# Eight small SBUF regions placed ahead of the load ring in a decode kernel of gated attention and MLP

## The chip, the cores and the metric

The kernel runs on one core of one Trainium2 chip. The metric is the device time of one execution in microseconds (us); the time before is the median of three runs. A profile of one further execution gives the span, from the first to the last instruction, and what each engine and each DMA queue did in it.

## What is computed

One token of 1024 values goes through two branches, and a gate mixes them. Branch A is attention over a cache: 32 query heads in 4 groups share 4 key and value heads, and each of these has 65,536 cached positions of 128 values. Branch B is a small gated MLP. All inputs are bf16. With its shapes filled in, and helper names shortened, the reference is:

```python
x = A_x                                            # [1, 1, 1024]
g = sigmoid((x * gate_w).sum(-1, keepdims=True))

q = (x @ wq).reshape(1, 1, 32, 128).transpose(0, 2, 1, 3)
k = repeat(k_cache, 8, axis=1)                     # k_cache, v_cache: [1, 4, 65536, 128]
v = repeat(v_cache, 8, axis=1)
p = softmax(einsum('bhqd,bhkd->bhqk', q, k) * 128 ** -0.5)
o = einsum('bhqk,bhkd->bhqd', p, v)
a = o.transpose(0, 2, 1, 3).reshape(1, 1, 4096) @ wo

z = gelu(einsum('bsd,df->bsf', x, w_in))           # w_in: [1024, 3584]
z1, z2 = z[..., :1792], layernorm(z[..., 1792:])
h = einsum('ts,bsf->btf', w_sp, z2) + b_sp
b = einsum('bsf,fd->bsd', z1 * h, w_out)           # w_out: [1792, 1024]

out = g * a + (1 - g) * b
```

The keys and the values are 67 MB each, and with the weights 162 MB are read once. Nothing of it is used twice, so the kernel is a stream of loads with work on the engines beside it.

## The kernel before

**SBUF.** All SBUF data lie in one tensor, `arena` (L202), of 128 partitions. `region` (L188) hands out its space by name, in the order of the list at L193, each region rounded up to 16 bf16 elements (32 bytes). `ab` (L204) and `af` (L207) make bf16 and f32 views from a region's offset, so an edit of the list moves the regions and touches nothing else. The program that is built from it puts `arena` at byte 16,512 of every partition, behind 16,384 reserved bytes and four constants of 32 bytes each.

The first region is `RING`, five slots of 16,384 elements (32 KiB per partition each). All large loads land there. `KT` holds two transposed key pieces, `SC` two buffers of scores, `PSB` and `PTSB` the probabilities and their transposes. The rest is small: `QPAD` holds the queries in the form that TensorE takes as weights for the scores, `SEL` and `BM` are selection matrices for the outputs and the maxima, `ONES` and `ONEB` ones in f32 and bf16, `IDB` an identity, `DM` and `M16` belong to the maximum over the heads' rows.

**Loads.** `stream` (L302) is a list of 29 transfers, written out by hand from L339 to L361: wq, K, w_in, K, K, w_out, then K and V by turns, and the output weights wo in six pieces, the last one of them cut in three by `WO_CUT` (L357). Each transfer is 128 rows, one for each partition, of 2,048 to 65,536 contiguous bytes. `issue` (L376) puts a transfer on SP's queue as soon as what lay in its slots has been used; the DMA is at L389. SP issues in the order of the list, and the first two transfers are moved ahead of the program's start barrier (`R.ahead`). Four small loads (x, the gate's weights and two single values, by `small` at L285) go out on ACT's queue in the same way; those of x and of the gate land in `SC`, eight rows of 256 bytes each. The result goes out from `OROW` in eight rows of 256 bytes (L366); a store of the same bytes is issued earlier, before the last load.

**Keys.** For each K transfer `k_piece` (L496) runs four times per 16,384 positions: DVE transposes a quarter of a slot into `KT` (L502), and PE multiplies it with `QPAD`, eight matmuls of 512 columns into `scp` (through `mm`, whose calls have the lines L260 and L262). When the four are through, the slot is free for the next transfer in it. Two such steps fill `scp`, and `score_pair` (L518) copies it to `SC` and takes its maximum.

**Values.** ACT takes the exponentials (L534), DVE transposes them (L539, L542), and `pv_piece` (L544) multiplies them with a V transfer as it lies in the ring, 32 matmuls into `obt`. The `out_` functions scale and sort the result of a group into `OVZ`, where it is ready as weights for wo.

**End.** The last transfers are wo's. `wo_rows` (L689) and `wo_piece` (L705) multiply them piece by piece as they land (L712 for the last four pieces), with a few idle matmuls between (`spin`), DVE casts the sum (L775), and SP stores it.

The order of the instructions on each engine is that of the calls from L733 to L776. `Recorder` finds the waits between them from the names that each operation reads and writes; addresses play no part in it.

Of the kernel before, what the change touches and what calls it, by code (L numbers as in the profile page):

```python
# [138 lines left out]
def bass_gated_mix__gqa_block_cached__mixer_gmlp__decode_kernel(  # L139
# [22 lines left out]
    KC = D // 128  # L162
    FC = FH // 128
    OC = HQ * Dh // 128
# [3 lines left out]
    total = G * NP  # L168
# [3 lines left out]
    QP = 152  # L172
# [15 lines left out]
    def region(name, nbf):  # L188
        nonlocal cur
        OFF[name] = cur  # L190
        cur += (nbf + 15) // 16 * 16

    for name, n in [  # L193
        ("RING", NSUB * SUB), ("KT", NKT * 4096), ("SC", NSC * 2048), ("PSB", 2 * 1024), ("PTSB", 2 * 1024),
        ("QPAD", 4 * QP), ("IDB", 128), ("BM", 256), ("SEL", 16 * 32),
        ("M16", 32), ("MQ", 32), ("XT", KC), ("WB", 2), ("WBB", 4), ("ONEB", 128),
        ("MAXC", 2 * total), ("LP", 2 * total), ("COLS", 2 * 64), ("DM", 64), ("ONES", 256), ("QALL", 128), ("OVZ", 32 * OC + 31), ("E4Z", 128), ("MHALF", 4),
        ("YB", FC), ("OROW", QW),
    ]:
        region(name, n)  # L200
# [608 lines left out]
```

## Time and profile before

| what | value |
|---|---|
| median of three runs | 381.85 us (381.73 to 382.11) |
| span of the profiled execution | 380.3 us |
| time of the median run beyond that span | 1.55 us |
| PE busy | 235.1 us, 62% |
| DVE busy | 204.6 us, 54% |
| ACT busy, POOL busy | 23.3 us and 8.4 us |
| HBM read | 162.01 MB, 426 GB/s over the span |

The profile has one line for a group of instructions: the line of the code, the engine, the operation, what it writes and reads, how many there are, busy time, mean time of one, and the idle time of its engine just before them with what ended it. A "DMA share" is the mean busy share of the 16 DMA engines in a stretch; it can read a little over 1. Beside these views the trace keeps each single DMA packet with its queue, start, length in bytes and duration in whole ns. A row of a load is one packet.

### The profile page before, as it was taken

To read this page: it belongs to the slowest core of one execution; us is meant where nothing else is said; L and a number is where in the kernel's file an instruction comes from. 1 tells how busy PE (TensorE), PEld (TensorE's weight loads), DVE (VectorE), ACT (ScalarE), POOL (GpSimd) and SP (SyncE) were. 2 spreads that over 40 slices of the span, in tenths; PEclk is the share of its full clock that TensorE was granted. 3 is DMA by queue.
4 is the path that set the end of the run, shared out by engine and by line. 5 is a ranking of instruction groups with operands and counts; after the bars stand their busy time and mean duration, and the time that the engine had idled before them with its cause. 6 is when DMAs were issued, how large, how long until landed. Compare 5 with 4: busy or idle time off the path is not lost.

```text
span 380.3 us, 2581 instructions
## 1 busy us (share of the span) xinstructions
PE 235.1 (62%) x1449; PEld 58.1 (15%) x836; DVE 204.6 (54%) x162; ACT 23.3 (6%) x24; POOL 8.4 (2%) x37
## 2 busy tenths in 40 slices
PE   0061388458558924895788138952895884739378
PEld 0010011011111200122112001220121110212015
DVE  4011496778389525965892249745774882312020
ACT  1000000010420000002200000022000000220000
POOL 5000000000000000000000000000000000000000
PEclk9998599696859985998699859995899697958689
DMA  9999999999999999999999999999999999999996
GB/s 435 427 420 400 469 388 438 441 469 431 401 414 441 441 443 427 434 410 424 477 441 434 434 434 414 415 441 441 434 407 433 445 441 441 436 403 424 419 426 262
DMA packets 4254, 162.17 MB, mean 426 GB/s; under 512 B 532, under 2 KB 532, under 8 KB 788
## 3 DMA queue, kind: packets, MB, share of 16 engines
q1 hardware_dynamic: 4208, 162.01, 98.9%
q8 instruction: 9, 0.15, 0.2%
q10 hardware_dynamic: 36, 0.00, 0.0%
q14 instruction: 1, 0.01, 0.0%
HBM read 162.01 MB, written 0.00 MB: 426 GB/s over the span
## 4 chain that ended last, share of the span: by engine, by line
DMA 56%; PE 23%; DVE 18%; ACT 1%; issue 1%; SPq 0%; ACTq 0%; DVEq 0%
DMA arena<-in_A_k_cache_dram 34%; DVE arena L502 15%; DMA arena<-in_A_wo_dram 10%; DMA arena<-in_A_v_cache_dram 8%; PE scp L260 7%; PE scp L262 6%; DMA arena<-in_B_b_sp_dram 5%; PE obt L260 4%; PE obt L262 4%; DVE arena L539 1%; PE fbt L712 1%; PE fbt L660 1%; ACT arena L534 1%; SPq L389 0%; ACTq L288 0%
## 5 line engine op out<-in xcount | busy, mean ns | idle before, releaser
L502 DVE STREAM_TRANSPOSE arena<-arena 128x2048 f32<-128x2048 f32 x64 | 143.0, 2284 | 48.2 <-DMA arena<-in_A_k_cache_dram 32.7
L260 PE MATMUL scp<-arena 128*128 128x512 bf16 (+1 forms) x275 | 112.8, 429 | 87.7 <-DVE arena L502 86.3
L262 PE MATMUL scp<-arena 128*128 128x512 bf16 (+1 forms) x279 | 113.1, 427 | 0.0
L260 PE MATMUL obt<-arena 128*64 128x512 bf16 (+2 forms) x334 | 62.9, 419 | 17.5 <-DMA arena<-in_A_v_cache_dram 17.5
L262 PE MATMUL obt<-arena 128*64 128x512 bf16 (+2 forms) x334 | 62.2, 414 | 0.0
L260 PEld LDWEIGHTS scp<-arena 128*128 128x128 bf16 (+1 forms) x275 | 27.7, 104 | 200.1 <-issue 101.3
L539 DVE STREAM_TRANSPOSE arena<-arena 128x2048 bf16<-128x2048 bf16 x7 | 16.2, 2311 | 28.5 <-PE obt L262 26.4
L534 ACT ACTIVATE arena<-arena 128x2048 bf16<-128x2048 f32 x8 | 16.0, 2002 | 218.6 <-DVE arena L531 195.6
L260 PEld LDWEIGHTS obt<-arena 128*64 128x64 bf16 (+1 forms) x334 | 18.3, 113 | 70.7 <-issue 56.1
L519 DVE TENSOR_SCALAR_CACHE_REDUCE arena<-scp 128x2048 f32<-128x2048 f32 x8 | 18.3, 2292 | 16.0 <-PE scp L262 16.0
L580 PE MATMUL mbt<-arena 128*128 128x128 bf16 x16 | 1.9, 258 | 12.6 <-DVE arena L575 12.6
L542 DVE STREAM_TRANSPOSE arena<-arena 128x1024 bf16<-128x1024 bf16 x2 | 2.5, 1246 | 12.7 <-PE obt L262 12.7
L490 POOL COPY arena<-arena 32x32 bf16<-32x32 bf16 x16 | 3.2, 203 | 234.5 <-PE scp L262 209.7
L568 DVE RECIPROCAL arena<-mbt 128x1 f32<-128x1 f32 x4 | 0.6, 139 | 14.1 <-PE mbt L563 14.1
L531 DVE TENSOR_REDUCE arena<-mbt 128x1 f32<-128x32 f32 x4 | 0.8, 192 | 13.5 <-PE mbt L528 13.5
L437 PE MATMUL mbt<-arena 1*128 1x2 bf16 x1 | 0.2, 158 | 12.3 <-DMA arena<-in_B_b_sp_dram 12.3
L439 DVE COPY arena<-mbt 128x2 f32<-128x2 f32 x1 | 0.2, 160 | 12.3 <-PE mbt L437 12.3
L775 DVE CAST arena<-fbt 36x128 bf16<-36x128 f32 x1 | 0.3, 283 | 11.0 <-PE fbt L712 11.0
L432 PE MATMUL scp<-arena 8*128 8x1 bf16 x8 | 0.7, 199 | 8.7 <-DVE arena L427 8.7
L712 PE MATMUL fbt<-arena 128*32 128x128 bf16 x128 | 4.1, 220 | 0.1
L712 PEld LDWEIGHTS fbt<-arena 128*32 128x32 bf16 x128 | 3.6, 97 | 1.6 <-DMA arena<-in_A_wo_dram 0.8
L467 DVE CAST arena<-obt 97x1024 bf16<-97x1024 f32 x1 | 1.2, 1225 | 4.9 <-PE obt L262 4.9
(91 smaller groups left out, 54.2 us busy)
## 6 DMA issues: line engine op xcount, KB each, us to landing
arena<-in_A_k_cache_dram SPq DMA_DIRECT2D x6, 4096.0 KB, 33.1
arena<-in_A_v_cache_dram SPq DMA_DIRECT2D x2, 4096.0 KB, 26.0
arena<-in_B_w_in_dram SPq DMA_DIRECT2D x1, 7168.0 KB, 30.4
arena<-in_A_wo_dram SPq DMA_DIRECT2D x3, 2048.0 KB, 33.4
arena<-in_B_w_out_dram SPq DMA_DIRECT2D x1, 3584.0 KB, 21.5
arena<-in_A_wo_dram SPq DMA_DIRECT2D x1, 1280.0 KB, 30.3
arena<-in_A_wo_dram SPq DMA_DIRECT2D x1, 512.0 KB, 31.0
arena<-in_A_wo_dram SPq DMA_DIRECT2D x1, 256.0 KB, 30.8
```

The lines of the kernel that those rows point to most:

```text
L260: return e.matmul(*a, **kw)
L262: one = e.matmul(*a, **kw).ins
L467: P("DVE", lambda e: e.tensor_copy(psb[0:97, :], ob[0:97, :]), w=["psb", "ob"])
L490: P("POOL", lambda e, pb=pb: e.tensor_copy(vw(qpad, 24 + 32 * pb, [[QP, 4], [1, 8]], 32 * pb, 32), vw(qall, 8 * g, [[32, 4], [1, 8]], 32 * ...
L502: P("DVE", lambda e: e.transpose(ktb(i).bitcast(F32), sl[:, 4096 * p:4096 * (p + 1)].bitcast(F32)), r=keys[4 * p:4 * p + 4], w=[("kt", i % ...
L519: P("DVE", lambda e: e.tensor_scalar(scs(j), scp[:, :], 0.0, None, op0=ALU.add, op1=ALU.max, accum_out=maxc[:, j:j + 1]), w=[("sc", j % 2) ...
L534: P("ACT", lambda e: e.activation(psb2, scs(j), ACTF.Exp, bias=gcol(j // 2, K_NB), scale=SCALE, accum_out=lp[:, j:j + 1]), r=[("sc", j % 2 ...
L539: P("DVE", lambda e: e.transpose(ptsb2, psb2), r=["psb"], w=[("ptsb", 0), ("ptsb", 1)])
L542: P("DVE", lambda e: e.transpose(ptsb(n), ab("PSB", 1024, 1024 * (n % 2))), r=["psb"], w=[("ptsb", n % 2)])
L580: ins = e.matmul(mb[:, 0:128], sel[:, 128 * c:128 * (c + 1)], osc[:, 128 * c:128 * (c + 1)], start=(c == 0), stop=(c == 3))
L660: ins = e.matmul(fb[32 * b:32 * (b + 1), 0:QW], e4z[0:97, 31 - j:63 - j], part[0:97, QW * s:QW * (s + 1)], start=(first and s % (NW // 2) ...
L712: ins = e.matmul(fb[32 * b:32 * (b + 1), 0:QW], ovz[:, z:z + 32], sl[:, o:o + QW], start=False, stop=(i == 3 and c == 7), tile_position=(0 ...
```

## The change

Only the list of regions changes. Eight regions that stood behind the large ones now stand ahead of `RING`; the others keep their order.

```diff
     for name, n in [
+        ("QPAD", 4 * QP), ("SEL", 16 * 32), ("BM", 256), ("ONES", 256), ("IDB", 128), ("ONEB", 128), ("DM", 64), ("M16", 32),
         ("RING", NSUB * SUB), ("KT", NKT * 4096), ("SC", NSC * 2048), ("PSB", 2 * 1024), ("PTSB", 2 * 1024),
-        ("QPAD", 4 * QP), ("IDB", 128), ("BM", 256), ("SEL", 16 * 32),
-        ("M16", 32), ("MQ", 32), ("XT", KC), ("WB", 2), ("WBB", 4), ("ONEB", 128),
-        ("MAXC", 2 * total), ("LP", 2 * total), ("COLS", 2 * 64), ("DM", 64), ("ONES", 256), ("QALL", 128), ("OVZ", 32 * OC + 31), ("E4Z", 128), ("MHALF", 4),
+        ("MQ", 32), ("XT", KC), ("WB", 2), ("WBB", 4),
+        ("MAXC", 2 * total), ("LP", 2 * total), ("COLS", 2 * 64), ("QALL", 128), ("OVZ", 32 * OC + 31), ("E4Z", 128), ("MHALF", 4),
         ("YB", FC), ("OROW", QW),
     ]:
         region(name, n)
```

In bytes from the start of a partition (16,512 is the start of `arena`):

| region | before | after |
|---|---|---|
| QPAD | 221,312 | 16,512 |
| SEL, BM, ONES | 223,296; 222,784; 225,312 | 17,728; 18,752; 19,264 |
| IDB, ONEB, DM, M16 | 222,528; 224,544; 225,184; 224,320 | 19,776; 20,032; 20,288; 20,416 |
| RING | 16,512 | 20,480 |
| KT, SC, PSB, PTSB | 180,352; 196,736; 213,120; 217,216 | each 3,968 more |
| MQ to COLS | 224,384 to 224,928 | 640 to 896 more |
| QALL to OROW | 225,824 to 228,512 | as before |

The arena's size stays 212,352 bytes.

## The prediction

> **What bounds the kernel now.** I read the page's slices, its DMA queues and its chain first, then a table by stage, then the end of the timeline, and last the single DMA packets of the trace.
>
> ```profile
> span 380.3 us, 2581 instructions
> ...
> DMA  9999999999999999999999999999999999999996
> ...
> q1 hardware_dynamic: 4208, 162.01, 98.9%
> ...
> DMA 56%; PE 23%; DVE 18%; ACT 1%; issue 1%; SPq 0%; ACTq 0%; DVEq 0%
> ...
> L502 DVE STREAM_TRANSPOSE arena<-arena 128x2048 f32<-128x2048 f32 x64 | 143.0, 2284 | 48.2 <-DMA arena<-in_A_k_cache_dram 32.7
> ...
> arena<-in_A_k_cache_dram SPq DMA_DIRECT2D x6, 4096.0 KB, 33.1
> ```
>
> The DMA engines are busy in every slice but the last. SP's queue q1 alone takes 98.9% of 380.3 us, 376.1 us on each of 16 engines, for 162.01 MB. The chain of waits names PE and DVE for 41%, but the first line of it is still DMA, and L502, DVE's largest group, stands idle 32.7 us for K loads. K transfers of 4096 KB need 33.1 us from issue to landing where their bytes need 9.7 (4,194,304 bytes at 16 times the 27.1 bytes per ns of one engine, below): 23 us of that is queueing, so the next transfer is there before the last one is through.
>
> ```profile
> core 0: us, PE busy (x) PEld busy (x) DVE busy (x) ACT busy (x) POOL busy (x), PEclk, DMA share, GB/s
> 0.00:1.00 1.00, 0.00 (x0) 0.00 (x0) 0.00 (x0) 0.00 (x0) 0.18 (x4) 1.00 0.20 66
> 1.00:96.00 95.00, 46.24 (x276) 10.71 (x152) 51.11 (x58) 3.17 (x5) 5.75 (x21) 0.86 1.01 434
> 96.00:368.00 272.00, 178.74 (x1004) 42.32 (x529) 153.20 (x103) 19.06 (x18) 2.43 (x12) 0.83 1.00 431
> 368.00:378.00 10.00, 9.50 (x160) 4.77 (x147) 0.00 (x0) 1.02 (x1) 0.00 (x0) 0.83 0.88 366
> 378.00:380.30 2.30, 0.67 (x18) 0.32 (x12) 0.28 (x1) 0.00 (x0) 0.00 (x0) 1.00 0.01 1
> ```
>
> By stage the DMA share is 1.00 or 1.01 from 1 to 368 us while no engine passes 66%. So the kernel is one unbroken stream of 376 to 377 us, with 1.0 us ahead of it and some 2.4 behind it. The end hangs on it too:
>
> ```profile
> 373.69 1.79 PEld L712 LDWEIGHTS fbt<-arena 128*32 128x32 bf16 x64 [0.66 <-DMA arena<-in_A_wo_dram]
> ...
> 378.27 0.23 PEld L712 LDWEIGHTS fbt<-arena 128*32 128x32 bf16 x8 [0.18 <-DMA arena<-in_A_wo_dram]
> 378.79 0.28 DVE L775 CAST arena<-fbt 36x128 bf16<-36x128 f32 x1 [11.04 <-PE fbt L712]
> 379.10 0.31 SPq L366 DMA_DIRECT2D out_dram<-arena  x1
> ```
>
> PE's weight loads wait for the last pieces of wo (0.66 and 0.18 us), and what follows the last one is fixed. What the stream gains or loses, the end gains or loses nearly whole.
>
> **The packets.** Every row of a load is one packet: 29 transfers of 128 rows over 16 engines are 232 rows per engine. The shortest packets last 2418 ns for 65,536 bytes, 1213 for 32,768, 159 for 4,096, 84 for 2,048. The first two give 1205 ns for 32 KiB, 37.66 ns per KiB (27.2 bytes per ns). That leaves, beyond the bytes, 8.0, 7.9, 8.4 and 8.7 ns: a row costs its bytes plus some 8.5 ns, whatever its length. This bounds the whole case. A cost at each 4096-byte border inside a row would show in the slope or grow from 2 KiB to 64 KiB; it doesn't. Only a cost per row is left to be saved.
>
> **The change, part by part.**
> (1) No instruction, wait, byte or transfer is added or removed: 0.
> (2) The rows' start. The program puts the arena at byte 16,512 of each partition, which is 4 x 4096 + 128, and RING is its first region. The eight regions hold 608 + 512 + 256 + 256 + 128 + 128 + 64 + 32 = 1984 elements, 3968 bytes; RING goes to byte 20,480 = 5 x 4096. Slots are multiples of 4096 bytes, but for the last two pieces of wo (10,240 and 14,336 bytes into their slot), which come to multiples of 2048. Every row therefore starts on a multiple of 256, where it started 128 past one. The price of such a start stands in no single row, so I bound it. Nothing saved: the slope is already the same for all rows, 0. All saved: 232 x 8.5 ns = 1.97 us. Between these, the sixteen 256-byte packets of the first two small loads, written to SBUF 128 past a multiple of 256, last 18 ns each, 8.6 beyond their bytes (9.4); of the last store's eight, written to HBM, three last 15 ns, and the shortest 8192-byte instruction packets 307, some 5.7 beyond theirs. That is 3 ns less per packet for another destination: 232 x 3 = 0.70 us. And where rows are longer than their shortest they are so in steps of 4 ns (of 1664 rows of 64 KiB, 470 last 2418, 417 last 2422, 210 last 2426). I take one such step, 4 ns, which is nearest to the 3 ns of the small packets: 232 x 4 = 0.93 us less. Both ends stay for the range, 0 and 1.97.
> (3) The longer steps. From about 95 us on the median row of a transfer is mostly 11 to 13 ns beyond its bytes, where it was 8 to 9 before: some 4 ns on the 184 rows per engine of 23 transfers, 0.7 us. What makes them isn't seen; I count 0 and keep 0.7 either way out of the likeliest sum.
> (4) KT, SC, PSB and PTSB move by the same 3968 bytes as RING, so the engines' operands keep their distances; the eight small ones and MQ to LP get other addresses. No shape changes. By the nearest rows: the L502 transposes read slots at the same spacing as now; 64 at 2284 ns, 0 taken. Should each be 5% longer it is 64 x 114 ns = 7.3 us of DVE time, spread over 380 us in which DVE idles 176, hidden by the 23 us that K transfers lead; with that lead gone, a slot would be freed up to 0.46 us later per piece (four transposes of 114 ns), 16 pieces, 7.3 us at most. Gain: no way that it passes to the end, since DVE isn't waited for by the stream.
>
> Sum: 380.3 - 0.93 = 379.4 us of span. The median of the runs, 381.85, is 1.55 above the span of the profiled one; that part is left as it is: 380.92 us.
>
> [...]
>
> [...]
>
> **The rivals.**
> Nothing moves (1): the 8.5 ns are the packet's own and not its start's. For it: 474 of q1's 480 packets of 4 bytes last 9 ns, so even they have nearly 9 ns beyond their bytes. Against it: 15 and 307. Time 381.85.
> The equal starts cost (2): rows that begin on the same 4096 border in all partitions get one of the 4 ns steps more, at the DMA's write into SBUF. For it: the steps exist, in more than half of the 64 KiB rows, unexplained. Against: the rows share one offset, 128, already now, so they have been in step all along. Price: 232 x 4 = 0.93, 382.78; with two steps 383.71. It decides from the point where the shortest 64 KiB packet or the usual one is 2422 or more and the small packets don't get shorter.
> The transposes get slower (3), by (4): below 5% it is hidden, 381.85, at the price of the whole 7.3 us 389.2. Only the changed addresses speak for it; the unchanged distances against it.
>
> **How the numbers follow.** A difference under about 0.2%, 0.76 us, can't be told from none here: the border is 381.09 below and 382.61 above. Chances: the forecast, 3 to 8.5 ns less per row, 0.54 (its own range 379.88 to 381.15; 0.47 of it beyond the border, 0.07 within); nothing moves 0.27 (0.26 within, 0.01 faster by the steps of (3)); equal starts cost 0.14 and slower transposes 0.05, all slower. So faster 0.48, same 0.33, slower 0.19. The predicted time is 380.9. The range goes from 379.8, all of the constant gone, to 382.9, one step more on every row: some 0.03 is left out below and 0.12 above.
>
> **What would show it.** Right, if q1's share of the span times the span falls from 376.1 to about 375.2 us per engine; the shortest packets fall by the same few ns at every length (2418 to 2414, 84 to 80); the sixteen 256-byte packets into SBUF go from 18 to 14 or 15; L502's 2284 ns and the 4208 packets stay, and the last wait for wo remains PE's. Wrong: if these stay and the time moves, the cause is elsewhere, in the longer steps or the engines; if packets shrink and the time doesn't, the stream has gaps, to be seen as a DMA share under 1.00 between 1 and 368 us; if the 64 KiB packets shrink by more than 8.5 ns, the slope has changed, and the reading that rows pay nothing per 4096 bytes was false.

## The result

| | before | after |
|---|---|---|
| median of 15 runs | 381.85 us (381.64 to 382.11) | 381.03 us (380.78 to 381.37) |
| span of the profiled execution | 380.3 us | 379.5 us |

The ratio of the runs is 0.9981, with a 95% interval of 0.9974 to 0.9987: 0.82 us less, faster by just about the 0.2% that was named as the border.

The page of the changed kernel, in the lines that were shown of the one before (slices, DMA queue, chain, L502, K loads):

```profile
span 379.5 us, 2579 instructions
...
DMA  9999999999999999999999999999999999989996
...
q1 hardware_dynamic: 4208, 162.01, 99.0%
...
DMA 64%; PE 19%; DVE 16%; issue 1%; ACTq 0%; SPq 0%; DVEq 0%
...
L502 DVE STREAM_TRANSPOSE arena<-arena 128x2048 f32<-128x2048 f32 x64 | 143.0, 2284 | 47.7 <-DMA arena<-in_A_k_cache_dram 33.3
...
arena<-in_A_k_cache_dram SPq DMA_DIRECT2D x6, 4096.0 KB, 33.1
```

Packets, bytes and transposes are what they were: 4208, 162.01 MB, 64 at 2284 ns. The queue's time fell with the span, from 98.9% of 380.3 to 99.0% of 379.5. The chain now gives DMA 64% instead of 56%, which is no 8% more of DMA: between two K loads the chain can go by the transfer or by the transposes and matmuls that ran beside it, and here it took the transfer more often (K loads are 40.9% of it, 33.5% before).

By stage (columns: stretch, its length, each engine's busy time, granted TensorE clock, DMA share, GB/s) and at the end:

```profile
1.00:96.00 95.00, 45.60 (x278) 10.62 (x153) 51.19 (x58) 3.17 (x5) 5.78 (x21) 0.86 1.01 436
96.00:368.00 272.00, 177.86 (x1010) 42.33 (x536) 153.22 (x103) 19.06 (x18) 2.45 (x12) 0.83 1.00 432
368.00:378.00 10.00, 9.25 (x164) 4.99 (x147) 0.07 (x1) 1.02 (x1) 0.00 (x0) 0.83 0.82 339
```

```profile
372.86 1.79 PEld L712 LDWEIGHTS fbt<-arena 128*32 128x32 bf16 x64 [0.66 <-DMA arena<-in_A_wo_dram]
...
377.41 0.23 PEld L712 LDWEIGHTS fbt<-arena 128*32 128x32 bf16 x8 [0.17 <-DMA arena<-in_A_wo_dram]
377.93 0.28 DVE L775 CAST arena<-fbt 36x128 bf16<-36x128 f32 x1 [10.89 <-PE fbt L712]
378.24 0.31 SPq L366 DMA_DIRECT2D out_dram<-arena  x1
```

The DMA share is as full as before and the rate is higher by 2 and 1 GB/s in the two long stretches. At the end the pieces and their waits are nearly the same, only earlier: the last weight load starts at 377.41 us instead of 378.27, 0.86 us earlier, and waits 0.17 us for the same piece of wo (0.18 before). Nearly all of the difference lies in the stream ahead of it, whose last row ends at 377.07 us instead of 377.82, 0.75 earlier.

The single packets say where. The stream, from the start of the first row to the end of the last, went from 376.83 to 376.07 us, 0.76 less. All durations in the next block are in ns; "longer" rows are those that last 3 to 39 ns over the shortest row of their length, a few much longer ones (40 ns and more; before, 16 of the 25 are in the first transfer) are kept apart, and sums are per engine.

```
                                    before   after
shortest row of 65,536 bytes          2418    2418
rows at 2418, of 1664                  470    1530
shortest row of 2,048 bytes             84      84
rows 3 to 39 ns over their shortest   1698      64   of 3712
sum over the shortest, under 40 ns     677      49
sum of the rest (25 rows each)        1006     949
256-byte packets into SBUF at 18 ns     16      15   of 16
```

No row got shorter than the shortest had been. What went away is the steps: 0.63 us of the stream's 0.76. The few very long rows give 0.06 more; the last 0.07 is not in the rows' durations. In all runs below, rows are measured against these same shortest ones, those of the kernel before; in some of the runs a few rows (25 of 3712 at most) are 2 or 3 ns under them.

### The profile page after: what moved, and what is told of

It is laid out like the page before. It is cut to its first block, busy times and chain, and to the rows that moved or that the text cites. A ratio compares the mean times of both kernels' runs of the same rounds, so it can differ in the third digit from the quotient of the medians.

```text
span 379.5 us, 2579 instructions
## 1 busy us (share of the span) xinstructions
PE 232.7 (61%) x1447; PEld 57.9 (15%) x836; DVE 204.7 (54%) x162; ACT 23.3 (6%) x24; POOL 8.4 (2%) x37
## 3 DMA queue, kind: packets, MB, share of 16 engines
q1 hardware_dynamic: 4208, 162.01, 99.0%
HBM read 162.01 MB, written 0.00 MB: 427 GB/s over the span
## 4 chain that ended last, share of the span: by engine, by line
DMA 64%; PE 19%; DVE 16%; issue 1%; ACTq 0%; SPq 0%; DVEq 0%
DMA arena<-in_A_k_cache_dram 41%; DVE arena L502 14%; DMA arena<-in_A_wo_dram 10%; DMA arena<-in_A_v_cache_dram 8%; DMA arena<-in_B_b_sp_dram 5%; PE scp L262 5%; PE scp L260 5%; PE obt L260 4%; PE obt L262 4%; PE fbt L712 1%; DVE arena L539 1%; PE fbt L660 0%; ACTq L288 0%; SPq L389 0%; DVE arena L575 0%
## 5 line engine op out<-in xcount | busy, mean ns | idle before, releaser
L502 DVE STREAM_TRANSPOSE arena<-arena 128x2048 f32<-128x2048 f32 x64 | 143.0, 2284 | 47.7 <-DMA arena<-in_A_k_cache_dram 33.3
L260 PE MATMUL scp<-arena 128*128 128x512 bf16 (+1 forms) x273 | 110.9, 424 | 88.6 <-DVE arena L502 87.1
L262 PE MATMUL scp<-arena 128*128 128x512 bf16 (+1 forms) x279 | 111.7, 422 | 0.5 <-issue 0.5
```

The lines of the kernel that those rows point to most:

```text
L260: return e.matmul(*a, **kw)
L262: one = e.matmul(*a, **kw).ins
L502: P("DVE", lambda e: e.transpose(ktb(i).bitcast(F32), sl[:, 4096 * p:4096 * (p + 1)].bitcast(F32)), r=keys[4 * p:4 * p + 4], w=[("kt", i % ...
```

## The experiments

These readings stood against each other. A: the steps come from a row that starts off a 256-byte border. B: it is 4096 that counts, as the change's words have it. C: it is the small regions' new places. D and E, once A held: the steps need the engines' work in SBUF beside the DMA, or they come from the DMA side alone.

**128 unused bytes ahead of the ring, nothing else.**

```diff
     for name, n in [
+        ("PAD", 64),
         ("RING", NSUB * SUB), ...
```

> The only edit to the kernel before: 128 unused bytes ahead of the ring, so that every region moves by 128 bytes and rows start at 16,640 = 65 x 256, which is no multiple of 512 or 4096. Theory A (the 4 and 8 ns steps of the rows come from a start off a 256-byte border): about 60 rows of 3712 are 3 to 39 ns over their shortest, as in the changed kernel (64; 1698 before), and the ratio to before is 0.998 as there, some 381.0 us. Theory B (the border that counts is 4096): still some 1700 such rows, ratio 1.000. Theory C (moving the small regions away from behind the ring did it): 1700 rows, ratio 1.000.

Measured: 380.93 us, ratio 0.9979 (0.9970 to 0.9988); 164 longer rows; all that rows last over their shortest, the cases from 40 ns on left out, sums up to 0.14 us per engine (0.68 before, 0.05 after the change). Below, the second figure in us is always this sum. The ratio is that of the change; of the rows, some hundred more than expected stayed long, all but a handful of them before 170 us. B and C fall: rows start at 65 x 256, on no border of 512 or more, and the eight regions stand behind the ring in their old order.

**Four regions ahead, rows at a multiple of 2048.**

```diff
+        ("QPAD", 4 * QP), ("BM", 256), ("DM", 64), ("M16", 32),
         ("RING", NSUB * SUB), ...
```

> QPAD, BM, DM and M16 ahead of the ring, rows from 18,432 = 9 x 2048 (a multiple of 256 and 2048, not of 4096). Theory A (256): about 60 long rows, ratio 0.998. Theory B (4096): some 1700 long rows, ratio 1.000. Theory C (small regions): in part, since four of the eight are moved.

Measured: 381.03 us, 0.9980 (0.9971 to 0.9989), 74 longer rows, 0.05 us. As A says.

**Seven of the eight ahead, DM left behind.** The diff is against the changed kernel; DM goes back to its old place.

```diff
-        ("QPAD", 4 * QP), ("SEL", 16 * 32), ("BM", 256), ("ONES", 256), ("IDB", 128), ("ONEB", 128), ("DM", 64), ("M16", 32),
+        ("QPAD", 4 * QP), ("SEL", 16 * 32), ("BM", 256), ("ONES", 256), ("IDB", 128), ("ONEB", 128), ("M16", 32),
         ("RING", NSUB * SUB), ...
```

> Seven of the eight regions ahead of the ring, DM left behind, so rows start at 20,352, 128 past a multiple of 256, as far off as before. Theories A and B: some 1700 long rows, ratio 1.000, 381.85 us. Theory C (the place of the small regions): near the changed kernel, ratio 0.998, whatever the rows do.

Measured: 381.82 us, 1.0000 (0.9991 to 1.0009), 1697 longer rows, 0.68 us. This is the change with 64 elements taken out of it, and the gain is gone with them; C falls a second time.

**The ring at 20,480 behind other regions.**

```diff
+        ("OVZ", 32 * OC + 31), ("SEL", 16 * 32), ("QALL", 128), ("E4Z", 128), ("COLS", 2 * 64), ("MQ", 32),
         ("RING", NSUB * SUB), ...
```

> The ring at 20,480 as in the changed kernel, but with other regions ahead of it (OVZ, SEL, QALL, E4Z, COLS and MQ; of the eight only SEL). Theories A and B: about 60 long rows, ratio 0.998. Theory C: no gain, ratio 1.000.

Measured: 380.89 us, 0.9977 (0.9968 to 0.9987), 120 longer rows, 0.10 us. What fills the space made no difference here.

**64 unused bytes, and 32.** The edit is that of the first experiment with ("PAD", 32) and ("PAD", 16).

> 64 unused bytes ahead of the ring: rows start at 16,576, 192 past a multiple of 256 (a multiple of 64). Theory A (any start off a 256-byte border makes the steps, by the bytes of a second, partly used block): 1500 to 1900 rows over their shortest by 3 to 39 ns, ratio 1.000. Theory A2 (a multiple of 64 is enough): about 60 rows and 0.998; but the kernel before is a multiple of 128 and has 1698, so A2 is only kept for the case that 128 is a special distance.

> 32 unused bytes ahead of the ring: rows start at 16,544, 160 past a multiple of 256 and a multiple of 32 only. Theory A: as with 64 bytes, 1500 to 1900 long rows and ratio 1.000. Theory A3 (the finer the start, the more pieces a row's ends are written in): longer steps than 4 and 8 ns or more rows with them, ratio 1.001 to 1.003.

Measured: 381.92 us, 1.0004 (0.9994 to 1.0013), and 381.84 us, 1.0000 (0.9991 to 1.0009). Starts at 192 and 160 past a border cost as much as those at 128: 0.70 and 0.66 us per engine against 0.68. The sizes of the steps differ, though: at 192 the commonest are 2 ns (1423 rows, which the count from 3 ns on leaves out; hence only 1054 longer rows against the 1500 to 1900 expected) and 9 ns (521), at 160 they are 1, 8 and 4, with 1466 longer rows, just under the 1500 to 1900 expected. A2 and A3 fall by the times. Every row here is a multiple of 256 bytes long, so a row that starts off a border also ends off one: the runs don't tell which of the two ends costs.

**Loads alone.** All work on PE, DVE and ACT is left out, and on POOL all but one memset; the 29 transfers go into the same slots in the same order, each waiting for the one before it in its slots, and zeros are stored.

```diff
     R = Recorder()
-    P = R.op
+
+    def P(eng, fn, r=(), w=(), dma=None):
+        if dma is not None or eng in () or "orow" in w and eng == "POOL":
+            R.op(eng, fn, r, w, dma)
...
-    P("DVE", lambda e: e.tensor_copy(orow[0:W0 + NW, :], fb[0:W0 + NW, 0:QW]), w=["orow", "fb"])
-    store()
+    P("SP", lambda e: e.dma_start(out[0, 0].rearrange("(q n) -> q n", n=QW), osrc),
+      r=["orow", "xr", "gr", "wsp", "bsp"] + [("slot", x) for x in range(NSUB * SUB // GRAN)], w=["out"], dma="out")
```

> The kernel before without any work on PE, DVE, ACT and POOL beyond one memset: all loads in the same order into the same slots at 16,512 and on, each waiting only for the load before it in its slots, then the store of zeros. Theory D (the steps come from the engines' accesses to SBUF beside the DMA's writes of partly filled blocks): under 100 rows of 3712 are 3 to 39 ns over their shortest. Theory E (they come from the DMA side alone, such as 16 engines that have drifted out of step): over 1000 such rows, from some 60 us on. The stream itself stays at 376 to 377 us in both.

Its page (span, busy engines, and the queue):

```profile
span 378.5 us, 61 instructions
## 1 busy us (share of the span) xinstructions
POOL 0.4 (0%) x5
...
q1 hardware_dynamic: 4208, 162.01, 99.3%
```

No engine works beyond a few memsets, and the steps are all there: 1774 longer rows, 0.70 us, in number from some 70 us on as in the whole kernel. The stream is 375.54 us, a little under the 376 to 377 expected. D falls. The run also shows how close the kernel is to its loads: one execution took 379.82 us, 2.0 less than the whole kernel with all its matmuls, transposes and exponentials.

**Loads alone, with 128 unused bytes ahead.**

> The run with loads alone once more (no work on PE, DVE, ACT and POOL beyond one memset), with 128 unused bytes ahead of the ring, so rows start at 16,640 = 65 x 256. Theory A (the start off a 256-byte border): under 150 rows of 3712 are 3 to 39 ns over their shortest (1774 at 16,512), and the stream is 0.5 to 0.7 us shorter than its 375.5 us. If the steps need something else of the DMA side: over 1000 such rows still.

```profile
span 377.6 us, 61 instructions
...
q1 hardware_dynamic: 4208, 162.01, 99.4%
```

91 longer rows, 0.05 us. The stream went from 375.54 to 374.74 us, 0.80 less (0.65 of it steps), a little beyond the 0.5 to 0.7 expected; the one execution took 378.92 us, 0.90 less. These are two single executions on two chips, on which the kernel before took 381.82 and 381.83 us. So the gain is the loads' own (0.80 us of stream here, 0.76 in the whole kernel), and it needs no work of the engines.

**Where the steps set in.** In the kernel before there are few until some 60 us (56 of the 425 rows that start by then, against 41 of 426 after the change), though its rows are as far off the border from the first on. Two more runs of the loads alone, at 128 past the border, in other orders:

```diff
     issued = [0]
-    used = set()
+    used = set(place)
     owner = {}
+    stream.sort(key=lambda t: (t[2].shape[1] != 16384, -t[2].shape[1]))
+    stream[:] = [(k, (i % 2) * VB, src) for i, (k, o, src) in enumerate(stream)]
...
```

> Loads alone, rows at 128 past a 256-byte border, all transfers in another order and by turns into two halves of the ring: first the eight with rows of 32 KiB (up to 77 us), then those of 64 KiB, then the rest. Where the steps set in: theory F (the transfers that take every second 32 KiB of their source start them): within the first transfers, before 30 us. Theory G (time: the 16 engines have to drift apart first): from some 60 to 70 us, as in the kernel before. Over 1000 long rows in all by both.

The second has -t[2].shape[1] as its key.

> The same with all transfers of 64 KiB rows first (13 of them, up to some 252 us), then 56 KiB, then 32 KiB. Theory F: few steps until some 270 us, where the rows of 32 KiB begin. Theory G: steps from some 60 to 70 us.

Measured, as the number of longer rows among all rows that start in a stretch:

```
us          0-20     20-40     40-60     80-100   140-170   200-220   250-280   320-350
l3         0/257     0/271   110/257     85/130     0/192    25/128     0/208   152/241
l4         1/130    31/142    13/128     20/137    56/195    61/128   163/280   261/401
```

By F the first order should have had steps within 30 us; it had none in 40. By G they should set in at 60 to 70 us and stay; in the first order they come at 40, are gone from 140 to 170, and are back from some 310. In the second they grow slowly. Both fall. Over the whole stream there are 1120 and 1679 longer rows. What decides whether a row off the border takes a step stays open.

## Why the prediction was right, and where it wasn't

**The bound: right.** The stream lost 0.76 us, the time 0.82, and the waits at the end kept their sizes.

**No cost per 4096 bytes inside a row: right.** The shortest rows of every length are unchanged, so the slope is; and rows on multiples of 256 or 2048 that are none of 4096 gain what those on 4096 do.

**The term for the rows' start, part (2): its place was wrong, its size too large by half.** The prediction took 4 ns per row out of the 8.5 ns that each row costs beyond its bytes, and named as proof that 2418 would become 2414, 84 become 80, and 18 become 14 or 15. None of that happened: 2418, 84, and 18 in 15 of 16. By its own signs this is the case "the cause is elsewhere, in the longer steps". The time of all q1 packets fell from 376.19 to 375.50 us per engine, not to about 375.2. The 8.5 ns are there on a border of 256 too, so they belong to the packet, as the first rival had it, though that rival's time, 381.85, did not follow. The comparison of 18 ns into SBUF with 15 ns into HBM said nothing about alignment: already in the trace of before, the eight packets of the earlier store, into HBM as well, last 18 ns (seven) and 25.

**The longer steps, part (3): this was the term.** It was rightly sized, 0.7 us, and counted at 0 because its cause wasn't seen. It measures 0.63 us in the whole kernel, 0.54 to 0.65 in the other pairs of runs whose rows start on and off a border. Spread over 232 rows it is 2.7 ns per row where part (2) had 4; so the forecast of 380.9 came out 0.13 us below the median by a term put into the wrong place and too large. That it came so near is luck in part: the case that came true, the 8.5 ns the packet's own and the steps of part (3) gone, had been given a chance of 0.01. The steps of 4 ns had been taken as a unit for the price, and were the price itself.

**The operands' addresses, part (4): right.** L502 stays at 2284 ns, and the two runs that split the ring's start from the regions' places agree.

**The rivals.** "Nothing moves" is out by the interval, which ends at 0.9987. "The equal starts cost" had the sign reversed: rows on one border took the steps away. "The transposes get slower" didn't occur.

**The border and the slope.** That a start on a multiple of 256 bytes is the one that counts was the author's assumption, which no row of the trace of before showed. The runs agree with it: 65 x 256 is enough (a sum of 0.14 us per engine over the shortest rows), and 128, 192 and 160 past a border are not (0.68, 0.70 and 0.66 us). A start off it has no fixed price on every row: the shortest rows are the same on the border and off it (2418 ns after the change and before), some rows take steps and others none, and in this order of the loads the sum hardly changes with the distance. The one slope of all rows was read as leaving nothing to save but a cost per row. The shortest rows run at that slope, 27.2 bytes per ns, after the change too, and the 0.2% was in the rows that take longer than these.

## What to carry to other kernels

Where one stream of loads is the bound, look at the spread of its packets' durations at one length before looking at their shortest: here the shortest gave no room, and the gain was in the 46% of rows that were a few ns over it. With such a bound it is worth placing the ring of loads on a multiple of 256 bytes: here it gave 0.2%, and 128 unused bytes did as much as the new order of the regions (0.9979 against 0.9981). When a term of a sum is seen in the trace but not explained, it belongs into the forecast with a chance and not at zero.

## Unexpected on the hardware

The steps come and go over stretches of tens of us (none in 192 rows from 140 to 170 us of one order, 152 of 241 from 320 to 350), with no engine at work, so neither access by the engines, nor time alone, nor the transfers' row length alone decides them. Their sizes depend on the distance from the border (4 and 8 ns at 128, 2 and 9 at 192, 1, 4 and 8 at 160), their sum hardly (0.68, 0.70 and 0.66 us per engine), while another order of the loads at the same 128 changed it (0.49 in the first one).
